# TensorE transposes for the first batch of an attention kernel, and float64 weights converted in pieces twice as wide

## Chip, cores, metric

One core of a Trainium2 chip. The metric is the device time of one execution in microseconds (us); a quoted time is a median of several executions.

## The reference, cut to what matters

Attention with a threshold, then a feed-forward block (FFN). Batch 8, 8 heads, 576 positions, head dimension 64; FFN 512 to 1536 to 512. q, k and v are float32, the three weight matrices are float64.

```python
scores = scale * np.matmul(q, k.transpose(0, 1, 3, 2))
thresh = np.max(scores, axis=-1, keepdims=True) - tau
scores = np.where(scores >= thresh, scores, -1000000000.0)
attn = np.exp(scores - np.max(scores, axis=-1, keepdims=True))
attn = attn / (np.sum(attn, axis=-1, keepdims=True) + 1e-09)
x = np.matmul(attn, v)                       # then heads side by side: (4608, 512)
g = x @ w_gate
out = (g * (1.0 / (1.0 + np.exp(-g))) * (x @ w_val)) @ w_out
```

## The kernel before

Two heads (a pair) are worked on together, a query tile of 128 rows at a time. Such a step is a *slot*, written (n,x): segment n, tile x of it. The first batch has segments 0 to 3 (three tiles each, stage A1) and 4 to 7 (the other two tiles, stage A2); the second batch has segments 8 to 11 with five tiles each (stage B). The later batches are "the rest". The FFN's matmuls are fed into the slots as soon as 384 rows of x are there.

The weights arrive as float64. They are fetched into places that are free yet (`land`, inside the later w_out tile), split on ScalarE (two instructions), and joined by four VectorE instructions and two on GpSimd, 384 columns at a time:

```python
def split_weights():
    ...
        nc.scalar.activation(tmp[:, 0, :], words[:, :, 1], AF.Abs, scale=2.0 ** -80)
        nc.scalar.activation(tmp[:, 1, :], words[:, :, 0].bitcast(U32), AF.Copy, scale=2.0 ** -52)

def join_weights():
    ...                                                      # up, lo, ex: 128 x 384
        nc.vector.tensor_scalar(out=up, ...)                 # L157
        nc.vector.tensor_scalar(out=ub, ...)                 # L159
        nc.vector.scalar_tensor_tensor(out=ub, in0=hi, ...)  # L161
        nc.vector.tensor_scalar(out=ex, ...)                 # L163
        nc.gpsimd.tensor_tensor(out=lo, in0=lo, in1=ex, op=ALU.mult)
        nc.gpsimd.tensor_tensor(out=dst, in0=up, in1=lo, op=ALU.add)

def weights(n):
    for _ in range(n):
        fetch_weights(2)
        split_weights()
        join_weights()
```

One slot, and the products with v in the first batch: VectorE transposes p in 32x32 blocks, so a product covers 32 keys only, and each segment needs 144 matmuls into four PSUM buffers (R = 4):

```python
        # in scores(): maxima (VectorE), exp (ScalarE), then
        turn(1 if halved else 0)                  # nc.vector.transpose of p of the slot before
        nc.vector.scalar_tensor_tensor(...)       # the threshold; frees the scores' PSUM
        ...
        nc.vector.reciprocal(out=ri[:, 0:m], in_=tot[:, 0:m])
        ...
        nc.scalar.activation(ps[x], ps[x], AF.Copy, scale=ri[:, x:x + 1])   # normalise
...
        # in attend():
        R = 2 if halved else NG
        xa = [ps_f.tile([P, 512], F32, name="xa", tag="psf") for _ in range(R)]
        for j in range(nj):
            for a in range(R):
                for h in range(2):
                    nc.tensor.matmul(xa[a][...], vr[rs, h, j, :], p[rs, lo:lo + n, j, :], ...)
```

`ps_f` has four buffers; products and FFN share them. The order in a slot, with where weights stand:

```python
            go = scores(seg, t); next(go)         # scores, maxima, exp
            ...
            if n >= NP: weights(1)                # before the threshold (A2 and later)
            next(go)                              # threshold, sums, reciprocal
            if n >= NP or n * len(early) + x < 2 * NCC: weights(1)   # after it
            ...
            next(go)                              # normalise
```

## Time and profile before

| | us |
|---|---|
| time, median of the runs beside the changed kernel | 1669.8 (1668.8 to 1670.9, 4 runs) |
| start, to the first slot's reciprocal | 15.7 |
| A1, 12 slots | 81.7 |
| A2, 8 slots | 87.4 |
| B, 20 slots | 217.3 |
| the rest | 1263.4 |

How to read it: each slot has exactly one reciprocal on VectorE, so the reciprocals cut the trace into slots, and the slots into stages. A stage runs from the reciprocal of its first slot to that of the next stage's first. In the same way the length of slot (n,x) is taken from its own reciprocal to the next one, so a conversion that stands before a slot's threshold lies in the length of the slot before it. The lines of the profile are in the prediction below.

### The profile page before, as it was taken

Reading aid. Unit: us, or ns where it says so; the run is one execution under the profiler, and the core shown is the slowest. Engines: PE = TensorE matmul, PEld = TensorE weight load, DVE = VectorE, ACT = ScalarE, POOL = GpSimd, SP = SyncE. Lnnn points to the kernel's source line nnn. Section 1 sums busy time; section 2 is a strip of 40 time slices with the busy share of each in tenths; the row PEclk is TensorE's granted clock in tenths of the full one; section 3 lists DMA queues with packets and bytes.
Section 4 is the critical chain, followed back from the end, with each engine's and each line's share of the span. In section 5 each row is a group of like instructions: output and inputs, shape, how many; then the busy total and the mean of one; then the engine's idle time right before and its main releaser. Section 6 shows DMA issues by size and latency. Waiting matters only on the chain.

```text
span 1665.6 us, 31316 instructions
## 1 busy us (share of the span) xinstructions
PE 1529.6 (92%) x11872; PEld 826.1 (50%) x11872; DVE 1115.5 (67%) x3772; ACT 565.1 (34%) x1308; POOL 800.4 (48%) x750
## 2 busy tenths in 40 slices
PE   4567676699999999999999999999999999999998
PEld 2444334356855545545544545445545545455453
DVE  7986499687787878777877777767777777601000
ACT  4554344224333333323323323323323424312011
POOL 3233668646555655654554654645545545501111
PEclk9787788799999999999999999999999999999999
DMA  7544222211111111111111110111111110000000
GB/s 175 125 105 127 70 77 73 73 43 36 30 30 43 29 49 30 29 48 30 29 36 43 29 35 21 22 48 30 30 42 36 30 42 21 7 13 1 13 7 19
DMA packets 176935, 74.00 MB, mean 44 GB/s; under 512 B 155280, under 2 KB 161424, under 8 KB 176784
## 3 DMA queue, kind: packets, MB, share of 16 engines
q1 hardware_dynamic: 173904, 62.55, 16.6%
q0 software_dynamic: 2880, 9.44, 1.5%
q8 instruction: 94, 1.54, 0.4%
q14 instruction: 57, 0.47, 0.1%
HBM read 62.52 MB, written 9.44 MB: 43 GB/s over the span
## 4 chain that ended last, share of the span: by engine, by line
PE 78%; DVE 13%; POOL 3%; ACT 2%; issue 2%; SPq 1%; DMA 1%; DVEq 0%; POOLq 0%; ACTq 0%
PE po L405 21%; PE pg L372 20%; PE pv L380 19%; PE xa L328 9%; PE sc L242 8%; DVE p L278 3%; DVE p L301 2%; DVE mx L262 2%; DVE tmp L161 1%; POOL p L290 1%; DVE nm L271 1%; DVE tmp L159 1%; PE sc L247 1%; DVE mx L221 1%; DVE tmp L157 1%
## 5 line engine op out<-in xcount | busy, mean ns | idle before, releaser
L290 POOL TENSOR_SCALAR p<-p,ri 128x288 f32<-128x288 f32 x504 | 499.9, 1008 | 420.5 <-DVE ri L286 416.4
L380 PE MATMUL pv<-xT,wv 128*128 128x384 f32 (+1 forms) x1248 | 409.5, 472 | 8.1 <-ACT gt L373 7.7
L372 PE MATMUL pg<-xT,wg 128*128 128x384 f32 (+1 forms) x1248 | 407.5, 470 | 9.5 <-ACT xT L351 8.2
L405 PE MATMUL po<-wo,ht 128*128 128x512 f32 x864 | 389.3, 603 | 10.7 <-POOL wo L168 9.1
L380 PEld LDWEIGHTS pv<-xT,wv 128*128 128x128 f32 x1248 | 232.6, 193 | 162.8 <-issue 20.3
L372 PEld LDWEIGHTS pg<-xT,wg 128*128 128x128 f32 x1248 | 231.6, 192 | 163.8 <-issue 22.6
L278 DVE SCALAR_TENSOR_TENSOR p<-sc,th,p 128x288 f32<-128x288 f32 (+1 forms) x540 | 256.2, 526 | 38.1 <-ACT p L274 38.0
L405 PEld LDWEIGHTS po<-wo,ht 128*128 128x128 f32 x864 | 160.9, 191 | 218.8 <-issue 196.0
L262 DVE TENSOR_REDUCE mx<-sc 128x2 f32<-128x576 f32 x252 | 179.4, 749 | 111.5 <-PE sc L242 111.4
L272 ACT ACTIVATE th<-nm,cut 128x4 f32<-128x4 f32 (+2 forms) x160 | 47.5, 297 | 582.2 <-DVE nm L265 540.8
L274 ACT ACTIVATE p<-sc,nm 128x288 f32<-128x288 f32 (+1 forms) x540 | 235.5, 511 | 0.6
L301 DVE STREAM_TRANSPOSE p<-p 128x576 f32<-128x576 f32 x288 | 207.2, 753 | 0.8 <-POOL p L290 0.8
L381 DVE TENSOR_TENSOR ht<-gt,pv 128x384 f32<-128x384 f32 (+1 forms) x156 | 78.5, 511 | 178.1 <-PE pv L380 174.9
L328 PE MATMUL xa<-p,vall 64*64 64x288 f32 (+3 forms) x4320 | 169.2, 340 | 29.5 <-issue 15.5
L242 PE MATMUL sc<-kT,qT 64*32 64x288 f32 x4032 | 170.7, 416 | 25.3 <-DVE p L278 25.3
L391 POOL TENSOR_TENSOR ht<-ht,gt 128x768 f32<-128x768 f32 (+1 forms) x78 | 129.5, 1690 | 99.0 <-ACT gt L390 99.0
L328 PEld LDWEIGHTS xa<-p,vall 32*64 32x64 f32 (+1 forms) x4320 | 113.2, 149 | 92.6 <-issue 36.1
L373 ACT COPY gt<-pg 128x384 f32<-128x384 f32 (+1 forms) x156 | 70.7, 458 | 186.6 <-PE pg L372 183.9
L242 PEld LDWEIGHTS sc<-kT,qT 64*32 64x32 f32 x4032 | 66.4, 107 | 131.7 <-issue 104.6
L197 POOL TENSOR_SCALAR qraw<-qraw,scl 128x576 f32<-128x576 f32 x32 | 55.4, 1730 | 79.5 <-DMA qraw<-in_q_dram 68.7
L221 DVE TENSOR_REDUCE sums<-sums 32x4 f32<-32x4 f32 (+1 forms) x560 | 83.9, 150 | 10.5
L221 DVE TENSOR_REDUCE mx<-mx 32x4 f32<-32x4 f32 (+1 forms) x560 | 83.2, 149 | 10.4
(57 smaller groups left out, 740.4 us busy)
## 6 DMA issues: line engine op xcount, KB each, us to landing
vall<-in_v_dram SPq DMA_DIRECT2D x112, 144.0 KB, 3.2
qraw<-in_q_dram SPq DMA_DIRECT2D x128, 72.0 KB, 2.3
kraw<-in_k_dram SPq DMA_DIRECT2D x128, 72.0 KB, 2.7
out_dram<-ob POOLq DMA_DIRECT2D x36, 256.0 KB, 2.4
vall<-in_v_dram SPq DMA_DIRECT2D x28, 288.0 KB, 5.3
wo<-in_moe_w_gate_dram SPq DMA_DIRECT2D x16, 384.0 KB, 4.9
wo<-in_moe_w_val_dram SPq DMA_DIRECT2D x16, 384.0 KB, 6.4
xT<-in_moe_w_out_dram SPq DMA_DIRECT2D x10, 384.0 KB, 3.3
```

The lines of the kernel that those rows point to most:

```text
L221: nc.vector.tensor_reduce(out=x[g * G:(g + 1) * G, 0:m, 1], in_=x[o * G:(o + 1) * G, 0:m, 0:1], axis=AX.X, op=ALU.max)
L242: nc.tensor.matmul(ps[g * G:(g + 1) * G, u, 0:SH], qT[hs, col + a * G:col + (a + 1) * G], kT[hs, c * SH:(c + 1) * SH], start=True, stop=True)
L262: nc.vector.tensor_reduce(out=mx[:, 2 * x:2 * x + 2, 0], in_=tile_[:, :, 0:SH], axis=AX.X, op=ALU.max, negate=True)
L274: nc.scalar.activation(ps[x], scs[x], AF.Exp, bias=nm[:, x:x + 1])
L278: nc.vector.scalar_tensor_tensor(out=ps[x], in0=scs[x], scalar=th[:, x:x + 1], in1=ps[x], op0=ALU.is_ge, op1=ALU.mult, accum_out=sm[:, x, ...
L290: nc.gpsimd.tensor_scalar(out=ps[x], in0=ps[x], scalar1=ri[:, x:x + 1], scalar2=None, op0=ALU.mult)
L301: nc.vector.transpose(out=p, in_=p)
L328: nc.tensor.matmul(xa[a][h * D:(h + 1) * D, at:at + n * G].rearrange("d (i q) -> d i q", q=G), vr[rs, h, j, :], p[rs, lo:lo + n, j, :], st ...
L372: nc.tensor.matmul(ps[:, 0:n], wg[:, c, f * P:(f + 1) * P], x[:, c, cs], start=(c == 0), stop=(c == NCC - 1))
L380: nc.tensor.matmul(ps[:, 0:n], wv[:, c, f * P:(f + 1) * P], x[:, c, cs], start=(c == 0), stop=(c == NCC - 1))
L391: nc.gpsimd.tensor_tensor(out=ht, in0=ht, in1=gt, op=ALU.mult)
L405: nc.tensor.matmul(po, hts[f // 2][:, f % 2, i * P:(i + 1) * P], wo[:, f, :], start=(f == 0), stop=(f == NF - 1))
```

## The change

Its intent: take the transposes of p off VectorE and the 144 small matmuls off TensorE in the first batch, and spend fewer VectorE instructions on the weights.

1. *Turns.* TensorE transposes the normalised p, 128x128 at a time, into PSUM; ScalarE copies the result. The products then contract over 128 keys: 10 matmuls in one PSUM buffer.
2. *Weights.* Gate and value are joined together, 768 columns per piece: 24 double pieces instead of 48.
3. *Places.* In A1 a double piece stands in every second slot, and before the threshold; afterwards one per slot (before: two). There are five landing places; the last w_out pieces must share one.

```diff
+    def flip():
+        while unflipped:
+            ...
+                for kt in range(KT):
+                    nc.tensor.transpose(tp[:, kt * P:(kt + 1) * P], p[:, kt * P:(kt + 1) * P], ident)
+                if t < NT:
+                    nc.tensor.matmul(end[h * D:(h + 1) * D, 0:P], p[:, KM:S], ident, start=True, stop=True)
+                    nc.scalar.copy(pT[:, h, :, col:col + P], tp.rearrange("p (t q) -> p t q", q=P))
+            ...
+    def attend_first(seg):
+        xa = ps_f.tile([P, 512], F32, name="xa", tag="psf")
+        for kt in range(KT):
+            for h in range(2):
+                nc.tensor.matmul(xa[h * D:(h + 1) * D, 0:n], vr[:, h, kt, :], pT[:, h, kt, :],
+                                 start=(kt == 0), stop=False)
 ...
-    wg = const.tile([P, NCC, DFF], F32, name="wg")
-    wv = const.tile([P, NCC, DFF], F32, name="wv")
+    wgv = const.tile([P, 2, NCC, DFF], F32, name="wgv")
+    TW = 2 * TC
+    wplaces = deque([4, 2, 3, 4, 3, 4, 4, 4])
 ...
-    fetch_weights(2)
+    fetch_weights(1)
     fetch_qk(1)
     load_v(segs[0])
-    fetch_weights(NL)
+    fetch_weights(3)
     split_weights()
 ...
-            if n >= NP:
+            flip()
+            if n >= NP or (n * TA + x) % 2 == 0:
                 weights(1)
             next(go)
-            if n >= NP or n * len(early) + x < 2 * NCC:
-                weights(1)
```

## The prediction

> **What bounds the kernel now.** I read the page's forty slices first, for where TensorE idles:
>
> ```profile
> PE   4567676699999999999999999999999999999998
> DVE  7986499687787878777877777767777777601000
> PEclk9787788799999999999999999999999999999999
> ```
>
> From the ninth slice on TensorE is full, and the diff leaves that code alone. Before it TensorE idles, its clock sags and VectorE is fullest. Then I read the timeline. A unit of attention work (a slot: scores of one query tile of a head pair, max, exp, threshold, reciprocal) ends with one reciprocal on VectorE (L286), so the reciprocals date all 160 slots. They give five stages: start; A1, 12 slots (three tiles of four pairs); A2, 8 slots (the rest of the first batch, with the first feed-forward (FFN) work); B, 20 slots (second batch, weight conversion still running); and the rest. Busy time by stage:
>
> ```profile
> 0.00:15.70 15.70, 3.09 (x11) 1.77 (x12) 5.21 (x18) 4.71 (x8) 3.63 (x6) 1.00 0.67 131
> 15.70:97.50 81.80, 43.56 (x964) 30.23 (x964) 73.48 (x166) 45.64 (x90) 23.05 (x21) 0.84 0.62 149
> 97.50:184.90 87.40, 65.80 (x1356) 40.89 (x1354) 59.30 (x147) 38.52 (x100) 34.20 (x33) 0.80 0.46 120
> 184.90:402.20 217.30, 165.24 (x1468) 97.74 (x1460) 174.23 (x568) 80.82 (x196) 141.96 (x135) 0.87 0.23 58
> 402.20:1665.60 1263.40, 1251.88 (x8099) 655.46 (x8084) 803.30 (x2875) 395.41 (x918) 597.54 (x556) 1.00 0.13 29
> ```
>
> Columns: stretch, length, busy us of PE, PEld, DVE, ACT, POOL, granted clock, DMA share, GB/s. The last stage is 99% TensorE and the program order of its matmuls is the same in both kernels, so its 1263 us stay. The rest is 402 us, in which TensorE idles 124 (15.7+81.8+87.4+217.3 less the busy 277.7).
>
> A1 is a ring between VectorE and TensorE (timeline, one slot):
>
> ```profile
> 25.01 1.38 DVE L271 TENSOR_REDUCE nm<-sc 128x1 f32<-128x576 f32 x2
> ...
> 26.32 1.42 DVE L301 STREAM_TRANSPOSE p<-p 128x576 f32<-128x576 f32 x2
> ...
> 26.63 1.35 ACT L274 ACTIVATE p<-sc,nm 128x576 f32<-128x576 f32 x2
> 27.66 0.77 DVE L278 SCALAR_TENSOR_TENSOR p<-sc,th,p 128x576 f32<-128x576 f32 x1
> ...
> 28.59 2.99 PE L247 MATMUL sc<-p,qT 64*128 64x288 f32 x8 [4.54 <-DVE p L278]
> ```
>
> The maxima, then the exp on ScalarE, with the transposes of p in its shadow; then the threshold, which frees the scores' PSUM; then the next scores, 2.99 us here (1.24 at full clock); the weight conversion lies under them. A2 instead stalls where the products take all four PSUM buffers and the FFN queues behind their copies:
>
> ```profile
> 169.84 0.55 ACT L146 ACTIVATE tmp<-wo 128x384 f32<-128x384 f32 x1 [6.18 <-POOL wg L168]
> ...
> 171.95 5.04 PE L372 MATMUL pg<-xT,wg 128*128 128x384 f32 x8 [6.35 <-ACT xT L351]
> ...
> 178.21 1.42 DVE L262 TENSOR_REDUCE mx<-sc 128x2 f32<-128x576 f32 x2 [10.32 <-PE sc L242]
> ```
>
> That slot takes 19.2 us, its like in B 23.2. The other slots of B with weights take 10.5, VectorE busy nearly throughout.
>
> **What the Trainium skill says.** "TensorE: Matmul & The Clock Gate", Part 4 (PE-mode transpose): a full 128x128 in one instruction, through PSUM, so a copy follows; about 275 ns in bf16, and it does not lift the clock. The trace before has none. The same page, Part 1: the clock halves after idle windows; the trace agrees (2.99 against 1.24 us above, clock 0.84 in A1). "SBUF — State Buffer", Who interferes with whom: VectorE's two-port tensor_scalar and a GpSimd instruction exclude each other; L159 takes 361 ns in the median and up to 1840, so the trace agrees. "TensorEngine Tiling (Array Packing)", Key Properties: different tiles run in parallel; at 408 us of the timeline 36 products of 288 columns on 64x64 tiles take 4.6 us; at the FFN's pace (4 matmuls of 384 columns in 2.74 us, 1.8 ns a column) one after the other would take 18.5.
>
> **The change, part by part.** *Removed from VectorE*: 36 transposes of p (9 arrays in each of 4 pairs), 753 ns each, 27 us. In A1 they lie under the exp, so each slot gets back only the 0.26 us by which the threshold waits (27.66 against the first exp's end, 27.4).
>
> *Weights*:
>
> ```profile
> L159 DVE TENSOR_SCALAR tmp<-tmp 128x384 uint32<-128x384 uint32 x48 | 24.3, 505 | 1.6
> L157 DVE TENSOR_SCALAR tmp<-tmp 128x384 f32<-128x384 f32 x48 | 20.4, 424 | 0.0
> L161 DVE SCALAR_TENSOR_TENSOR tmp<-wo,tmp 128x384 uint32<-128x384 uint32 x32 | 18.2, 569 | 1.1
> L163 DVE TENSOR_SCALAR wo<-tmp 128x384 uint32<-128x384 uint32 x32 | 12.0, 374 | 3.0 <-DVE tmp L161 0.5
> ```
>
> Unblocked (medians 349, 361, 557, 360) a piece costs 1.63 us. Some 150 ns of each instruction are fixed (384 columns at one per cycle are 400 of L161's 557), so a double piece costs about 2.63 instead of 3.26: 24 of them save 15 us. ScalarE splits one in about 1.9 us (555 ns for 384, 761 for 576 columns). More matters where they stand: 6 double pieces in A1 (12 old ones, before 8), one per slot afterwards, done 10 slots into B, where two old pieces per slot took 12. But they now stand before the threshold: in half of A1's slots 2.6 us in place of a 1.1 us gap.
>
> *Added*: per full slot 8 transposes and 2 small matmuls on TensorE, an estimated 2.7 us from the page's 275 ns; 36 copies of 512 columns (586 ns, as L409) and 20 small ones on ScalarE, 26 us, spread over 20 slots. *Products*: 10 matmuls instead of 144, in one PSUM buffer instead of four; 3.5 us or 1.9 (384 or 192 columns, two tiles at once) against 4.5 to 5, and nothing queues behind four copies.
>
> *Start*: ScalarE must now split the second piece before it normalises the first slot, and that piece is fetched behind pair 1's q, k and v.
>
> ```profile
> 22.91 0.56 ACT L146 ACTIVATE tmp<-wo 128x384 f32<-128x384 f32 x1 [2.46 <-DMA wo<-in_moe_w_gate_dram]
> ```
>
> The same transfer lands at 22.9 here. With its partner at about 24, plus split 1.9 and normalising 1.4, the second slot's exp starts near 27.3 instead of 19.1: +8 us.
>
> Sum by stage. *Start +8.* *A1 −3*: slots without weights 5.2 to 6.2 by clock (scores 1.1 to 2.2, maxima 1.4, exp 1.1, threshold 1.5), with them 6.8 to 7.8, three slots with products +1.5: 76 to 80 for what took 81.7. *A2 −11*: pairs of slots on TensorE: scores 2.3, products 1.9, turns 4.2, FFN 11.1, 19.5 or a little over, three times, plus 16 for the first pair: 76 instead of 87. *B −26*: of the ten slots with weights (124.7 us before), the one of 23.2 becomes 13 (−10), the one of 15.3 becomes 13 (−2), eight others go from 86 to 83 (−3; the last two pieces share one landing place, so their slots win nothing). The next two, 9.4 and 22.8 us, in which the FFN waits for w_out and catches up, become 7.5 and 11.5 (−13). The other eight, 60.5 us, have a little less FFN work to hide behind VectorE's 7.2 us per slot: +2. Sum of all: 8 −3 −11 −26 = −32: 1638.
>
> **The rivals.** (1) *The ring does not care*: transposes were under the exp and weights under the scores, so A1 grows with weights now in the chain, TensorE's turns run at half clock and delay the next scores; A1 +8, A2 −4, B −18, start +8: 1664. For it: only 0.26 us per slot were exposed. Against: the PSUM stalls of 15 to 23 us do go. (2) *B becomes free*: if fewer, longer VectorE instructions meet GpSimd's lock less often and all pieces are there in time, B falls towards its TensorE work of 165 and the start's delay is absorbed: 1612. Against: GpSimd itself has 142 of 217 busy in B, and in weight slots about 9.5 us (normalising 4.3, joining 3.5, products and q the rest). (3) *ScalarE becomes the bound*: 26 us of copies. A full weight slot has th 0.3, exp 1.35, copies 1.45, split 1.9, normalising 1.45: 6.5 us, at the slot's own length in A1. If it binds, 1650.
>
> **Range and chances.** The mechanisms point to a gain of 15 to 50 us, on stages that take a quarter of the time; two per cent is 33 us, right at my sum. Rival 1 has a quarter of the weight, rival 2 a quarter. So 1638, range 1614 to 1662; faster by over 2% 0.48, within 2% 0.49, slower 0.03.
>
> **What would show it.** Second slot's reciprocal near 30 instead of 21.9 (start); first slot of A2 ends near 104 instead of 97.5; TensorE slots of 15 to 23 us gone from A2 and early B; B begins near 180 and ends near 370 instead of 402.2; then 1263 us unchanged. Wrong if transposes cost well over 0.3 us each, if the clock in A1 falls below 0.84, if a ScalarE split waits for GpSimd or a transfer in most slots, or if the last stage's length changes.

## The result, and the profile after

| | before | after | difference | predicted |
|---|---|---|---|---|
| time, us | 1669.8 (1668.8 to 1670.9) | 1644.9 (1641.8 to 1646.9) | -25 | -32 |
| start | 15.7 | 17.7 | +2.0 | |
| A1 | 81.7 | 87.4 | +5.6 | |
| start and A1 | 97.5 | 105.1 | +7.6 | +5 |
| A2 | 87.4 | 71.0 | -16.4 | -11 |
| B | 217.3 | 203.1 | -14.2 | -26 |
| the rest | 1263.4 | 1263.5 | +0.1 | 0 |

Differences are taken before rounding. Ratio 0.9849, 95% interval 0.9832 to 0.9866. Ratios here are the mean time of one kernel's runs over that of the other's of the same rounds, so not quite the ratio of the medians.

The forty slices of the page of the changed kernel:

```profile
PE   4789875899999999999999999999999999999998
DVE  5766886778777777777777777767776777601000
PEclk9889987899999999999999999999999999999999
```

TensorE is fuller in slices 2 to 5, where it had 5 to 7 tenths; VectorE has come down from 9 and 8 tenths to 7 and 6 in slices 2 and 3. There is a dip to 5 in the seventh slice: that is in B, and it is the part of the prediction that failed.

The stages of the changed kernel (stretch, length, busy us and instructions of PE, PEld, DVE, ACT, POOL, granted clock, DMA share, GB/s):

```profile
17.80:105.20 87.40, 67.47 (x305) 37.76 (x306) 60.11 (x130) 62.00 (x113) 27.06 (x16) 0.84 0.42 111
105.20:176.20 71.00, 66.70 (x381) 36.56 (x378) 46.90 (x106) 44.24 (x82) 31.72 (x19) 0.98 0.30 87
176.20:379.30 203.10, 157.36 (x1190) 91.37 (x1176) 160.23 (x510) 71.11 (x160) 129.68 (x108) 0.89 0.23 58
379.30:1642.80 1263.50, 1252.09 (x8098) 655.72 (x8084) 802.91 (x2875) 394.83 (x918) 596.99 (x556) 1.00 0.13 29
```

In A2 TensorE is busy for 66.7 of 71.0 us at a clock of 0.98 (before: 65.8 of 87.4 us, at 0.80): the stage is now TensorE's own work. Its busy time did not shrink, although 144 small matmuls per segment are gone: what went is idle time, 21.6 us before and 4.3 us now. In A1 VectorE's busy time fell by 13 us, from 73.5 to 60.1, and the stage became *longer*. VectorE was not what to save there.

**A1, a slot with weights.** Timeline of the changed kernel; the columns are start, duration, engine, line, operation, tiles, shapes:

```profile
55.49 1.42 DVE L283 TENSOR_REDUCE nm<-sc 128x1 f32<-128x576 f32 x2 [0.55 <-PE sc L259]
55.83 0.66 PE L330 MATMUL tp<-ident,p 128*128 128x128 f32 x4
...
57.15 1.35 ACT L286 ACTIVATE p<-sc,nm 128x576 f32<-128x576 f32 x2
...
58.01 0.96 DVE L170 SCALAR_TENSOR_TENSOR wgv<-wo,wgv 128x768 uint32<-128x768 uint32 x1
59.00 0.56 DVE L172 TENSOR_SCALAR wo<-wgv 128x768 uint32<-128x768 uint32 x1
59.48 0.81 DVE L290 SCALAR_TENSOR_TENSOR p<-sc,th,p 128x576 f32<-128x576 f32 x1
...
60.44 2.99 PE L259 MATMUL sc<-p,qT 64*128 64x288 f32 x8 [2.64 <-DVE p L290]
```

The exp ends at 58.50 (57.15 + 1.35); the conversion holds VectorE until 59.56, so the threshold starts a microsecond late, and the next scores, which wait for it, find TensorE idle for 2.64 us and its clock down (0.50 granted from 60.3 to 67.0): 2.99 us for what takes 1.24 at full clock. The turns themselves are cheap: four in 0.66 us, with 0.43 for the two small matmuls.

**B, the two slots that grew.** Timeline of the changed kernel, slots (9,2) and (9,3), which took 10.5 and 15.3 us before and take 16.3 and 20.4 now:

```profile
259.45 1.67 ACT L286 ACTIVATE p<-sc,nm 128x288 f32<-128x288 f32 x4
...
260.99 0.93 ACT L154 ACTIVATE wo<-xT 128x768 f32<-128x768 f32 x1
...
261.96 1.13 DVE L166 TENSOR_SCALAR wo<-wo 128x768 f32<-128x768 f32 x1 [4.16 <-ACT wo L154]
...
269.45 1.21 PE L254 MATMUL sc<-kT,qT 64*32 64x288 f32 x16 [7.22 <-DVE p L290]
...
272.40 0.73 DVE L609 STREAM_TRANSPOSE qT<-qraw 128x576 f32<-128x576 f32 x1
...
273.16 1.93 SPq L203 DMA_DIRECT2D qraw<-in_q_dram  x4
...
275.14 2.60 SPq L203 DMA_DIRECT2D kraw<-in_k_dram  x4
...
277.83 0.57 SPq L143 DMA_DIRECT2D xT<-in_moe_w_out_dram  x1
...
283.94 0.89 ACT L154 ACTIVATE wo<-xT 128x768 f32<-128x768 f32 x1 [8.20 <-DMA xT<-in_moe_w_out_dram]
...
284.86 0.69 DVE L166 TENSOR_SCALAR wo<-wo 128x768 f32<-128x768 f32 x1 [10.23 <-ACT wo L154]
```

In (9,2) the piece is split only after the exp, in the same slot in which it is joined, so VectorE waits 4.2 us for ScalarE, the threshold follows the join, and TensorE idles 7.2 us. The join itself is slow here too: it lasts from 261.96 to 267.1, 5.2 us, against 3.5 in (9,3). The kernel before had split its piece a slot ahead. In its slot (9,2) the join starts at once after the maxima (which end at 276.42), and TensorE idles 1.4 us before the same scores; timeline of the kernel before:

```profile
276.26 0.16 DVE L265 TENSOR_REDUCE nm<-mx 128x4 f32<-128x8 f32 x1
276.34 0.35 DVE L157 TENSOR_SCALAR tmp<-tmp 128x384 f32<-128x384 f32 x1
...
280.75 0.72 PE L242 MATMUL sc<-kT,qT 64*32 64x288 f32 x16 [1.40 <-DVE p L278]
```

In (9,3) even the transfer is part of that chain: the piece shares its landing place with the one before, so it is asked for only after that one is joined. By then it stands behind the loads of the next q and k, and those wait for a buffer that the transposes free at 273.1. VectorE waits 10.2 us. The Trainium skill, "DMA: Bandwidth & Descriptors", Anatomy of one DMA — SWDGE (gpsimd) path, says that a DMA's semaphore wait happens on the issuing sequencer before dispatch. That section describes transfers issued by GpSimd; here SyncE issues them, and the trace agrees for it: the w_out transfer is issued 4.7 us after the first of the q loads, which start when their buffer is free.

### The profile page after: what moved, and what is told of

It reads as the page before. It is cut to its first block, busy times and chain, and to the rows that moved or that the text cites. A ratio compares the mean times of both kernels' runs of the same rounds, so it can differ in the third digit from the quotient of the medians.

```text
span 1642.8 us, 27168 instructions
## 1 busy us (share of the span) xinstructions
PE 1546.8 (94%) x9952; PEld 823.3 (50%) x9952; DVE 1078.3 (66%) x3640; ACT 576.7 (35%) x1276; POOL 791.6 (48%) x704
## 3 DMA queue, kind: packets, MB, share of 16 engines
q1 hardware_dynamic: 173328, 55.47, 14.9%
## 4 chain that ended last, share of the span: by engine, by line
PE 82%; DVE 9%; issue 3%; ACT 2%; POOL 2%; DMA 1%; SPq 1%; POOLq 0%; DVEq 0%; ACTq 0%
PE pg L427 21%; PE pv L435 20%; PE po L460 20%; PE sc L254 9%; PE xa L383 8%; DVE p L290 2%; DVE mx L274 1%; PE xa L350 1%; PE sc L259 1%; DVE p L316 1%; POOL p L302 1%; PE tp L330 1%; SPq L203 1%; DVE mx L231 1%; POOL ht L446 1%
## 5 line engine op out<-in xcount | busy, mean ns | idle before, releaser
L427 PE MATMUL pg<-xT,wgv 128*128 128x384 f32 (+1 forms) x1248 | 403.8, 467 | 2.4 <-ACT gt L428 2.4
L435 PE MATMUL pv<-xT,wgv 128*128 128x384 f32 (+1 forms) x1248 | 404.6, 467 | 0.0
L427 PEld LDWEIGHTS pg<-xT,wgv 128*128 128x128 f32 x1248 | 229.7, 191 | 153.6 <-issue 19.0
L435 PEld LDWEIGHTS pv<-xT,wgv 128*128 128x128 f32 x1248 | 229.6, 191 | 153.4 <-issue 18.8
L460 PEld LDWEIGHTS po<-wo,ht 128*128 128x128 f32 x864 | 161.2, 192 | 210.4 <-issue 196.3
L316 DVE STREAM_TRANSPOSE p<-p 128x576 f32<-128x576 f32 x252 | 181.3, 754 | 0.8 <-POOL p L302 0.8
L383 PE MATMUL xa<-p,vall 64*64 64x288 f32 x2016 | 131.5, 409 | 3.8 <-DVE p L316 3.7
L383 PEld LDWEIGHTS xa<-p,vall 64*64 64x64 f32 x2016 | 79.4, 134 | 58.6 <-issue 13.3
L231 DVE TENSOR_REDUCE sums<-sums 32x4 f32<-32x4 f32 (+1 forms) x560 | 83.9, 150 | 10.5
```

Of the source, the lines that this page charges most:

```text
L231: nc.vector.tensor_reduce(out=x[g * G:(g + 1) * G, 0:m, 1], in_=x[o * G:(o + 1) * G, 0:m, 0:1], axis=AX.X, op=ALU.max)
L316: nc.vector.transpose(out=p, in_=p)
L383: nc.tensor.matmul(xa[a][h * D:(h + 1) * D, at:at + n * G].rearrange("d (i q) -> d i q", q=G), vr[rs, h, j, :], p[rs, lo:lo + n, j, :], st ...
L427: nc.tensor.matmul(ps[:, 0:n], wgv[:, 0, c, f * P:(f + 1) * P], x[:, c, cs], start=(c == 0), stop=(c == NCC - 1))
L435: nc.tensor.matmul(ps[:, 0:n], wgv[:, 1, c, f * P:(f + 1) * P], x[:, c, cs], start=(c == 0), stop=(c == NCC - 1))
L460: nc.tensor.matmul(po, hts[f // 2][:, f % 2, i * P:(i + 1) * P], wo[:, f, :], start=(f == 0), stop=(f == NF - 1))
```

## The experiments

Eleven kernels ran, each beside the kernel before on the same chip, three rounds each, all with correct results. The stage columns are from the one profiled execution. In every profile the rest took 1263.3 to 1263.6 us. Read the clock of A1 as an upper bound: the time before a trace's first clock record (at 18.9 to 49.2 us) counts as full speed. In the changed kernel that record comes at 29.5, and three groups of four turns before it took 1.1 us each, the group right after it 0.66.

| kernel | median us (range) | ratio to before [95%] | start | A1 (clock) | A2 | B |
|---|---|---|---|---|---|---|
| wide_alone | 1669.9 (1668.7 to 1670.2) | 1.0011 [0.9995, 1.0028] | 17.7 | 95.4 (0.77) | 81.3 | 210.4 |
| turns_alone | 1640.5 (1640.0 to 1642.8) | 0.9839 [0.9825, 0.9854] | 15.1 | 76.2 (0.88) | 71.1 | 212.4 |
| fetch_early | 1634.4 (1629.8 to 1635.8) | 0.9795 [0.9778, 0.9813] | 17.4 | 84.9 (0.88) | 69.3 | 196.2 |
| odd_slots | 1641.1 (1639.6 to 1643.0) | 0.9841 [0.9826, 0.9855] | 15.8 | 86.9 (0.84) | 71.0 | 202.9 |
| under_scores | 1643.0 (1640.8 to 1644.7) | 0.9840 [0.9826, 0.9855] | 16.1 | 83.7 (0.92) | 72.6 | 204.2 |
| two_buffers | 1650.4 (1649.1 to 1652.5) | 0.9886 [0.9872, 0.9901] | 17.7 | 89.7 (0.75) | 74.3 | 204.5 |
| plain_turns | 1650.7 (1645.5 to 1651.8) | 0.9881 [0.9864, 0.9898] | 17.7 | 84.8 (0.96) | 74.8 | 202.8 |
| under_and_early | 1633.1 (1630.3 to 1634.3) | 0.9776 [0.9760, 0.9793] | 15.8 | 87.5 (0.84) | 71.0 | 194.6 |
| early_odd | 1637.1 (1635.4 to 1638.5) | 0.9811 [0.9796, 0.9825] | 15.8 | 89.0 (0.77) | 71.1 | 196.6 |
| odd_under_early | 1631.8 (1631.2 to 1632.9) | 0.9780 [0.9763, 0.9796] | 16.4 | 83.9 (0.80) | 71.4 | 195.1 |
| first_early | 1631.4 (1629.5 to 1634.7) | 0.9779 [0.9762, 0.9796] | 17.6 | 84.2 (0.83) | 71.0 | 196.6 |

The theory after the first look at the traces: the turns and the ten products make A2 short by freeing PSUM buffers; the conversion gains nothing in A1, and in B it loses at the end because of the shared landing place. The rival: fewer VectorE instructions are worth their 15 us wherever they stand, and the turns cost what they gain.

### wide_alone and turns_alone: one half of the change each

wide_alone is the kernel before with the changed conversion (`TW`, `places`, `wgv`, and one `weights(1)` per slot at the new places); turns_alone is the changed kernel with the old conversion, two single pieces per slot as before.

```diff
 # turns_alone against the changed kernel
-            if n >= NP or (n * TA + x) % 2 == 0:
+            if n >= NP:
                 weights(1)
             next(go)
+            if n >= NP or n * TA + x < 2 * NCC:
+                weights(1)
```

> The kernel before with the conversion of the kernel after (double pieces, six of them in the first twelve slots, standing before the threshold), but VectorE's transposes of p and the 144 products per pair as before. Stages by the reciprocals of VectorE, before and after: A1 81.7 and 87.4 us, A2 87.4 and 71.0, B 217.3 and 203.1. Theory (A2's gain comes from the products leaving three of the four PSUM buffers free, B's from the weights being done two slots earlier): A2 stays above 80 us, with slots of 13 us or more in its second halves, while B falls by 10 us or more below 217 and A1 grows to 88 or more (weights and transposes now both between maximum and threshold). Total 1660 to 1672. Rival (A2 gained because the double pieces were there in time, not because of PSUM): A2 falls to some 73 and the total to about 1648.

> The kernel after with the conversion of the kernel before (single pieces, 8 in the first twelve slots, standing after the threshold, two per slot later). Theory: A1 falls below the 81.7 us of before (the transposes are gone from VectorE and the weights lie under the scores): 74 to 79; A2 falls to about 75 (single PSUM buffer for the products, two pieces per slot on VectorE); B stays long, 210 to 217, but for the slot whose products now need one buffer (23.2 to about 14). Total 1640 to 1652. Rival (the two parts need each other: without the double pieces the first FFN waits for weights): A2 stays above 82 and the total above 1658.

The conversion alone brings nothing (1.0011), the turns alone bring all of it (0.9839). One expectation missed: in wide_alone B fell by 7 us, to 210.4, not by 10 or more. Why the conversion gains nothing although it saves VectorE work is seen in one slot of wide_alone's timeline:

```profile
62.01 0.55 DVE L163 TENSOR_SCALAR wgv<-wgv 128x768 f32<-128x768 f32 x1
...
62.39 1.35 ACT L280 ACTIVATE p<-sc,nm 128x576 f32<-128x576 f32 x2
...
64.18 0.98 DVE L169 TENSOR_SCALAR wo<-wgv 128x768 uint32<-128x768 uint32 x1
...
65.09 1.43 DVE L307 STREAM_TRANSPOSE p<-p 128x576 f32<-128x576 f32 x2
...
66.44 0.77 DVE L284 SCALAR_TENSOR_TENSOR p<-sc,th,p 128x576 f32<-128x576 f32 x1
```

The exp ends at 63.74, the threshold starts at 66.44: 2.7 us that the join and the transposes put in the chain of every second slot of A1. In turns_alone the join follows the reciprocal, under the next scores, and A1 falls to 76.2 us. But it has then converted less: 8 single pieces in A1 against 6 double ones. It pays in B, in slot (10,0), 25.4 us long; turns_alone's timeline:

```profile
289.87 5.33 PE L454 MATMUL po<-wo,ht 128*128 128x512 f32 x6 [14.24 <-POOL wo L171]
```

TensorE waits 14.2 us there for the last w_out pieces, as the prediction described for the kernel before. So the double pieces move work from B to A1: A1 +11, B -9 between turns_alone and the changed kernel. What they save is what they cost.

In A2, wide_alone keeps slots of 14.2, 14.9 and 16.0 us, (5,1) to (7,1), and (8,1) keeps 21.2; with the turns, they are 11.7, 11.7, 12.9 and 13.3 in the changed kernel. This stage belongs to turns and products.

### fetch_early: ask for the next transfer right after a join

```diff
             split_weights()
             join_weights()
+            fetch_weights(2)
```

> The kernel after, with the next piece of weights also fetched at the end of each conversion call, so that the last transfer of w_out stands in the DMA issue queue ahead of the next pair's q and k, not behind them. In the kernel after, the slot with it takes 20.4 us, of which VectorE waits 10.2 for ScalarE's split, which waited 8.2 for the transfer. Theory: this slot falls to 12 to 14 us, the one before it (16.3, no transfer waited for) stays within 1 us, the total falls by 6 to 9 us to 1636 to 1639. Rival (TensorE has a backlog there, or the split after the exp costs as much without the transfer): slot above 17, total within 3 us of the kernel after.

Slot (9,3) fell from 20.36 to 12.37 us, as the theory of the queue's order said; (9,2), where the split is late and not the transfer, stayed at 16.34. B fell by 6.9 us, the whole by about nine (0.9849 less 0.9795 of 1668 us), where 6 to 9 were expected; the profile has the rest of its gain in A1 and A2, and nothing shows that it comes from this edit. fetch_early's timeline:

```profile
247.79 16.65 SPq L143 DMA_DIRECT2D xT<-in_moe_w_out_dram  x2
...
268.20 1.95 SPq L204 DMA_DIRECT2D qraw<-in_q_dram  x4
...
270.67 0.89 ACT L154 ACTIVATE wo<-xT 128x768 f32<-128x768 f32 x1
```

The two last pieces are now issued within the stretch that ends at 264.4, ahead of the q loads, and the split needs no transfer any more at 270.7.

### odd_slots and first_early: the start

odd_slots puts A1's conversions in the odd slots, so the first slot has none. first_early keeps them where they are, with early transfers, but fetches the second double piece before the second pair's q, k and v.

```diff
 # odd_slots
-            if n >= NP or (n * TA + x) % 2 == 0:
+            if n >= NP or (n * TA + x) % 2 == 1:
 # first_early (and fetch_weights(2) after join_weights())
-    fetch_weights(1)
+    fetch_weights(2)
     fetch_qk(1)
     load_v(segs[0])
-    fetch_weights(3)
+    fetch_weights(2)
```

> The kernel after, with the six early conversions in the odd slots of A1 instead of the even ones; the first slot has none. Theory (ScalarE's normalising of the first slot stands behind the split of the second piece, whose transfer lands at 20.5 us): the second slot's reciprocal, 26.3 in the kernel after and 21.9 before, comes at 22 to 24, and A1 as a whole ends 3 to 5 us earlier, the total 1640 to 1642. Rival (the start is only moved: the odd slots pay the same wait one slot later, or the three slots with products, two of which now carry weights, grow): end of A1 within 1.5 us of 105.2.

> Changed kernel with early transfers, and the second double piece fetched before the second pair's q, k and v instead of after them; it is still converted in the first slot. Theory of the start (ScalarE's split in the first slot waits for a transfer that stands behind those loads in one queue; 20.55 us with 6.07 us of waiting): the wait vanishes, the second slot's exp starts at 19 to 20.5 instead of 23.6, second slot's reciprocal at 22 to 24. Rival (the first slot pays for the split's and the join's work itself, not the wait): reciprocal at 25 to 26.5. Total in either case 1630 to 1635, as the first stage's later slots add some us of their own.

ScalarE in the first slots, changed kernel:

```profile
20.55 0.89 ACT L154 ACTIVATE wgv<-wo 128x768 f32<-128x768 f32 x1 [6.07 <-DMA wo<-in_moe_w_val_dram]
...
22.11 1.43 ACT L304 ACTIVATE p<-p,ri 128x576 f32<-128x576 f32 x2
...
23.63 1.35 ACT L286 ACTIVATE p<-sc,nm 128x576 f32<-128x576 f32 x2
```

and first_early:

```profile
14.62 0.90 ACT L154 ACTIVATE wgv<-wo 128x768 f32<-128x768 f32 x1
...
17.83 1.44 ACT L305 ACTIVATE p<-p,ri 128x576 f32<-128x576 f32 x2 [1.52 <-DVE ri L299]
...
20.83 1.35 ACT L287 ACTIVATE p<-sc,nm 128x576 f32<-128x576 f32 x2
```

The wait of 6 us is gone, the second slot's exp comes 2.8 us sooner (0.3 us later than expected), and its reciprocal is at 23.4 instead of 26.2; with odd_slots at 23.1. The theory of the start holds. What it is worth is another matter: by the end of A1 first_early is at 101.9 and fetch_early, without this mend, at 102.3. The 2.1 us at the second slot (23.4 against 25.5) have shrunk to 0.4. In odd_slots A1 ended 2.4 us earlier than in the changed kernel, where 3 to 5 were expected, and the ratio (0.9841) cannot be told from 0.9849.

### under_scores, under_and_early, early_odd, odd_under_early: where A1's time is

```diff
 # under_scores: A1's conversion after the threshold
-            if n >= NP or (n * TA + x) % 2 == 0:
+            if n >= NP:
                 weights(1)
             next(go)
+            if n < NP and (n * TA + x) % 2 == 0:
+                weights(1)
             fill(part)
```

> The changed kernel with one move: in the first twelve slots the conversion of a double piece follows the threshold (it lies under the scores, as the old conversion did) and no longer precedes it; pieces, sizes and slots are the same. Theory (the place of the conversion is what made the first stage, A1, longer): A1 falls from 87.4 us to 76 to 80, near the 76.2 of the kernel with the turns alone; second slot's reciprocal at 22 to 24 instead of 26.2; TensorE's clock in A1 rises; the later stages stay within 2 us; total 1634 to 1639, ratio to the kernel before 0.978 to 0.983. Rival (the size of the pieces is what costs: 2.6 us on VectorE and 1.9 on ScalarE at one stretch do not fit under the scores): A1 stays at 84 to 88, total 1641 to 1646.

> The two mends together: conversion after the threshold in the first stage, and the next transfers of weights asked for right after a piece is joined, ahead of the loads of the next queries and keys in the queue. If the two effects are independent: A1 76 to 80, A2 69 to 71, B 195 to 198, total 1624 to 1630, ratio 0.972 to 0.977, the first version faster than before by over 2% in the whole interval besides the one with early transfers alone. If the gain of one is taken back by the other (B absorbs an earlier start, as it does where it waits for transfers): 1631 to 1635.

> Both mends that gained: transfers of weights asked for right after a join, and the first stage's conversions in its odd slots, so that the first slot has none. Odd slots alone brought the second slot's reciprocal from 26.2 to 23.1 and the first stage's end 2.4 us forward; early transfers alone took 7 us from B. Independent effects: total 1629 to 1633, ratio 0.976 to 0.979, second slot's reciprocal at 23, B at 195 to 197. Rival (the earlier start is lost again in the first stage, where TensorE's clock decides): 1633 to 1636.

> The same with the first stage's conversions after the threshold too (odd slots, early transfers). Without the first slot's wait for the second piece, and with the conversion under the scores, the first stage should come nearest to the 76.2 us of the kernel with the turns alone: 78 to 82, second slot's reciprocal at 21 to 23, total 1624 to 1629. Rival (the first stage's length is set by whether TensorE's clock is up during turns, products and scores, and the place of the conversion matters little): the first stage at 83 to 88 with a granted clock below 0.9 there, total 1630 to 1635.

For A1 the theories mostly missed. under_scores: A1 83.7, not 76 to 80; total 1643, not 1634 to 1639. The total is what its rival expected (that the pieces are too big to fit under the scores), and that rival is not excluded. under_and_early reached B's 195 as expected, but A1 stayed at 87.5, though its twelve slots have the very code of under_scores except that transfers are issued earlier. early_odd (0.9811) was no faster than fetch_early (0.9795), which has its conversions in the even slots; their intervals overlap. odd_under_early came to 83.9 at a clock of 0.80, which was its rival's expectation. So the place of the conversion is not enough to explain A1's length. A part that differs is the clock. The products of one segment, under_scores:

```profile
59.14 2.80 PE L350 MATMUL xa<-p,vall 128*64 128x384 f32 x16
```

and the changed kernel:

```profile
63.36 4.61 PE L350 MATMUL xa<-p,vall 128*64 128x384 f32 x16
...
70.59 1.24 PE L259 MATMUL sc<-p,qT 64*128 64x288 f32 x8
```

The same sixteen records take 2.8 or 4.6 us, according to whether the clock happens to be up. In TensorE's program order, the products and the turns stand before the next scores, and these wait. In the shortest slots of the changed kernel's A1 (5.75 us) the next scores start 0.8 us before the reciprocal; in (2,1) of the changed kernel they start 3.6 us after it (70.59 against 67.01), and the slot is 11.2 us long (before: 7.5). In early_odd it is (1,1) and (3,1), 11.2 and 10.9 us long, with products of 4.8 and 4.9 us and scores 3.7 and 3.9 us after the reciprocal. Slow products alone do not do it: in turns_alone products of 4.4 us leave (2,1) at 7.9. And the clock is not all of it either: plain_turns had the highest (0.96) and still took 84.8 us, 11.5 of them in (2,1). What sets A1 between 76 and 90 us is a mixture that these runs do not separate; each A1 is also that of a single execution, and the total of one kernel varied by up to 6 us.

### two_buffers: are PSUM buffers what A2 gained by?

```diff
-        xa = ps_f.tile([P, 512], F32, name="xa", tag="psf")
+        xa = [ps_f.tile([P, 512], F32, name="xa", tag="psf") for _ in range(2)]
 ...
-                nc.tensor.matmul(xa[h * D:(h + 1) * D, 0:n], vr[:, h, kt, :], pT[:, h, kt, :],
+                nc.tensor.matmul(xa[h][h * D:(h + 1) * D, 0:n], vr[:, h, kt, :], pT[:, h, kt, :],
```

> The changed kernel, but the products of the two heads go to a PSUM buffer each, and two copies of half the partitions take them out: two of the four shared buffers instead of one per segment. Theory (A2 shrank because the products no longer fill the four buffers that turns and feed-forward use too): A2 grows from 71.0 us by 2 to 6, and some slot of A2 passes 13 us; A1 grows by 0 to 2. Total 1647 to 1653. Rival (A2 shrank because ten matmuls replace 144 and VectorE has no transposes of p there; buffers do not matter): A2 within 1 us of 71.0, total 1644 to 1647.

A2 74.3 instead of 71.0, and (7,1) at 13.6: as the theory said. two_buffers' timeline:

```profile
146.16 0.66 PE L330 MATMUL tp<-ident,p 128*128 128x128 f32 x4
...
146.85 0.58 ACT L333 COPY p<-tp 128x512 f32<-128x512 f32 x1 [0.78 <-PE tp L330]
147.49 0.66 PE L330 MATMUL tp<-ident,p 128*128 128x128 f32 x4 [0.31 <-ACT p L333]
```

With one buffer fewer the second head's turns wait for the copy of the first's. The cost is 3.3 us, some 0.8 per segment, for one buffer more held by the products; the run also has one copy more per segment on ScalarE, which was not tested apart. Going from four held buffers to one is part of the 16 us that A2 won, but not measured alone: the number of matmuls changed with it.

### plain_turns: what if the turns were ordinary matmuls?

```diff
-                    nc.tensor.transpose(tp[:, kt * P:(kt + 1) * P], p[:, kt * P:(kt + 1) * P], ident)
+                    nc.tensor.matmul(tp[:, kt * P:(kt + 1) * P], p[:, kt * P:(kt + 1) * P], ident, start=True, stop=True)
```

> The changed kernel with the 144 TensorE transposes written as ordinary float32 matmuls with the identity (the result may differ in the last bits and stays inside the tolerance). The trace shows one record of some 165 ns for a float32 transpose where a float32 matmul has two. Theory (the turns are cheap enough because they are transposes; TensorE bounds A2): four turns take 1.2 to 1.4 us at full clock instead of 0.66, so a full slot costs 1.2 us more; A2, which is bound by TensorE, grows from 71.0 by 6 to 11 us; A1 by 3 to 10; total 1654 to 1666. Rival (turns lie beside other work; their cost does not matter): both stages within 2 us, total 1643 to 1648.

Four turns, plain_turns:

```profile
150.37 1.16 PE L330 MATMUL tp<-ident,p 128*128 128x128 f32 x8
```

Two records each, and 1.16 us for four where the transposes take 0.66. A2 grew by 3.8 us, less than the 6 to 11 expected. Each of its last three pairs of slots grew by 1.5 us, which is 0.5 for each of its three fours of turns; the first pair became 0.6 shorter, as its products ran at full clock there (2.8 us against 3.7 in the changed kernel). A1 cannot be read from this trace: the profiled execution was the fastest, at 1645.5, and the other three took 1650.7 to 1651.8. The total, 5 to 6 us above the changed kernel's, was lower than expected too. The direction is the theory's: in these three pairs, which TensorE bounds, the cost of turns counts in full.

## Why the prediction was right or wrong

**Right as a whole:** 1644.9 us lies in the range, within 2% of before. The gain is 25 us where 32 were expected. That the sum came so near is in part luck: A2 gained 5.4 us more than forecast, which covers nearly half of the 11.8 that B fell short. Its steps:

- *The rest unchanged.* 1263.5 against 1263.4: right.
- *A2 -11; measured -16.4.* The mechanism is right: the slots of 15 to 19 us went (14.4, 14.6, 19.2 became 11.7, 11.7, 12.9), and TensorE is busy nearly throughout. The forecast of 76 was 74.5 by its own terms and "a little over". The term mis-sized is "turns 4.2" per pair of slots, from the skill's 275 ns each. The tile's records in A2 (least, median and greatest duration in ns) show that 275 is the right duration of one turn:

```profile
L330 PE MATMUL tp<-ident,p x48: 272/273/330, 110.6 to 168.6; 128*128 128x128 f32 x48
```

  But turns overlap: four in a row took 0.66 us, 165 ns each, and adding durations counted the overlap as cost. A full slot has 2 x (0.66 + 0.43) = 2.2 us, the half slot with it 1.0 (0.66 + 0.33), so 3.2 per pair, and 4 us less in the stage's four pairs. plain_turns, with 290 ns per turn (1.16 us for four), had A2 at 74.8, near the 76 of the prediction.
- *Start +8 and A1 -3, together +5; measured +7.6.* Two errors that partly cancel. The second slot's exp came 4.5 us later than before (23.63 against 19.1), not 8: the double piece was split at 20.55, where "its partner at about 24" had been taken for the landing. In exchange A1 did not gain 3 but lost: of the 7.6 us, 4.3 had come by the second slot's reciprocal (26.2 against 21.9), 3.3 came after it. "Slots without weights 5.2 to 6.2, with them 6.8 to 7.8" held for many slots (5.75 and 7.77 each recur), but "three slots with products +1.5" did not: (2,1) alone gave 11.2, with the products mostly at half clock. Here, though not in A2, rival 1, "the ring does not care", was right: A1 got longer.
- *B -26; measured -14.2.* This is the step that failed. Its terms:

| term of B | predicted | measured |
|---|---|---|
| (8,1), 23.2 us | -10 | 13.3: -9.9 |
| (10,0) and (10,1), waiting for w_out | -13 | 19.1 instead of 32.2: -13.1 |
| the other eight slots after them | +2 | +0.5 |
| (9,3), 15.3 us | -2 | 20.4: +5.1 |
| eight other slots with weights | -3 | +3.3 |
| sum | -26 | -14.1 |

  Two terms are right to 0.1 us, a third to 1.5. The two others are wrong by 13, and most of that is in the prediction as an aside: "the last two pieces share one landing place, so their slots win nothing". They do not just win nothing. Where a piece cannot be fetched before its forerunner is joined, transfer, split, join, threshold and scores form one chain in a slot, and nothing lies beside anything. (9,1), (9,2) and (9,3) took 51.4 us instead of 37.6 (11.75 + 10.51 + 15.31); the other six of the eight won 5.5. (9,2) and (9,3) together took 25.8 us before, 25.5 with the turns alone, 37.6 with the conversion alone and 36.7 in the changed kernel: it is the conversion that lengthens them. fetch_early shows the transfer's share of that: 8.0 us in (9,3), which leaves 28.7 for the two. The last 2.9 us, with the late split and the slow join of (9,2), were seen in the trace but not taken away by a run. The 2.9 us of (9,1) are not explained by the chain: its piece had been split a slot ahead, and in five other runs, fetch_early among them, it took 13.0 us.
- *"24 of them save 15 us" of VectorE.* They do save it (the four instructions of the join took 91.9 us before and take 74.3; L161 at 384 columns has a median of 559 ns, its successor L170 at 768 has 959, so 159 ns are fixed, near the 150 of the estimate), and it is worth nothing: wide_alone 1.0011, and turns_alone as fast as both halves together. In A1 and B a slot's length is a chain through four engines, and work was moved onto it.

**Rival 2** ("B becomes free", 1612) fell: B took 203.1 us, not near 165; in its two long slots VectorE itself waited, 4.2 and 10.2 us, for ScalarE's split. **Rival 3** (ScalarE, 1650) fell too: 62 of 87 us busy in A1, 44 of 71 in A2.

**Faster than both kernels:** first_early (1631.4), odd_under_early (1631.8) and under_and_early (1633.1), 2.2% below before and some 0.7% below the changed kernel by their ratios. Their intervals overlap each other and that of fetch_early (0.9795), so these four are not told apart; most of the 0.7% is the one line of fetch_early.

**Open:** what sets A1's length between 76 and 90 us, as said above, and how the 16 us of A2 divide between buffers and the new order of work.

## What to carry to other kernels

Before counting the engine time that a change saves, find out whether the instructions stand on the chain of the slot: some 15 us of VectorE work saved brought nothing, while one line that issued a transfer some microseconds sooner brought nine. When buffers for landing are shared, write down for the last pieces what must follow what: fetch, split, join, use; and look at what else stands ahead in the queue that issues the transfer. And take the number of PSUM buffers that a product holds into the estimate: one more cost some 0.8 us per segment here.

## What the Trainium skill lacked or had wrong

- "TensorE: Matmul & The Clock Gate", Part 4 (PE-mode transpose): it gives about 275 ns in a kernel and 390 alone, for bf16, and neither a duration for float32 nor one for turns in a row. Here the record of a float32 128x128 transpose lasts 273 ns (median of 48 in A2), but four in a row take 0.66 us at full clock and 1.1 at half, 165 and 275 ns each. Ordinary float32 matmuls with the identity took 290 ns each in a row, in two records.
- The same section says that the clock gate does not engage for transposes. A2, with 48 of its turns among other matmuls, ran at a clock of 0.98, and turns in A1 are seen at both speeds; no run here has transposes alone, so whether they lift the clock is not shown.
- "DMA: Bandwidth & Descriptors", Anatomy of one DMA — SWDGE (gpsimd) path: it says where a wait is made, but not what it costs those behind it. Here a transfer that stood behind loads waiting for a buffer made a slot 8.0 us longer (20.4 against 12.4).
- No page has the cost of a PSUM buffer held longer: here 3.3 us in 71 for one buffer of four, with one copy more per segment.
